# Fixed program order in beats, and transposes by DMA, in a fused attention and MoE kernel

## The chip, the cores and the metric

The kernel runs on one core of a Trainium2 chip. The metric is the device time of one execution in microseconds (us).

Names: PE is TensorE (matmul), DVE is VectorE, ACT is ScalarE, POOL is GpSimd, SP is the engine that here only issues DMAs. PSUM is the memory into which PE writes its products; here it is eight banks, each a buffer.

## The reference, cut to what matters

```python
def phi(x):
    proj = np.einsum('bhsd,df->bhsf', x, w_phi)
    proj = proj - np.max(np.abs(proj), axis=-1, keepdims=True)
    return np.concatenate([np.exp(proj), np.exp(-proj)], axis=-1)
q_p, k_p = phi(q), phi(k)
kv = np.einsum('bhsf,bhsd->bhfd', k_p, v);  z = np.sum(k_p, axis=2)
x = einsum(q_p, kv) / (einsum(q_p, z) + 1e-06)     # then (batch*seq, heads*dim) = 4608 x 512
h = x @ w_in                                       # 4608 x 2048, the "first product"
g = np.where(h > 0.0, h, np.exp(np.minimum(h, 0.0)) - 1.0)
out = g @ w_out                                    # 4608 x 512, the "second product"
```

There are 8 batches of 8 heads, 576 positions, head size 64 and 128 features. The kernel works on "quads", 4 heads of one batch, so there are 16 quads. A "slot" projects quad n and finishes quad n-1. A "chunk" is 512 rows of the MoE part, one for each batch and a ninth for the left-over rows.

## The kernel before

The projection of four head parts goes into a PSUM bank `pk`. Two engines read the bank: DVE takes the maximum `m_k`, ACT takes two exps. The exps do not use the maximum; it goes into a separate factor for v (`em`).

```python
def project(xT, hh, m):
    pk = apsum.tile([P, 4, F], FP32, name="pk", tag="ap")      # one of 4 attention banks
    ... nc.tensor.matmul(pk[...], xT[:, 2 * hh + j, :], w_phi_rhs, ...)
    nc.vector.tensor_reduce(m[...], pk[...], op=ALU.max, apply_absolute_value=True)
    return pk[...]

def k_head(hh):
    pk = project(st["kT"], hh, st["m_k"])
    for sg in range(2):
        nc.scalar.activation(dst, pk, ACT.Exp, scale=1.0 - 2.0 * sg)     # dst is EK
```

A piece of the first product crosses four engines. The bank `ph` is free again only after `gT` has been written:

```python
def mm1(ch, jt):
    ph = mpsum.tile([P, CHUNK], FP32, name="ph", tag="mp")     # one of 4 MoE banks
    ... 4 x nc.tensor.matmul(ph, w_in_sb[...], xTs[ch][:, ct, :], ...)
    nc.scalar.activation(e_sb, ph, ACT.Exp)
    nc.gpsimd.tensor_scalar(u_sb, e_sb, -1.0, 1.0, op0=ALU.add, op1=ALU.mult)
    nc.vector.scalar_tensor_tensor(gTs[ch][:, jt, :], u_sb, 0.0, ph, op0=ALU.min, op1=ALU.max)
```

k, q and x are transposed on PE, nine 128x128 blocks at a time, and copied out of PSUM by DVE (`tr`, `kT`, `qT`, `xT`). The program emits the steps of a slot with MoE units among them, and a list scheduler decides the order of the instructions on each engine.

Of the kernel before, what the change touches and what calls it, by code (L numbers as in the profile page):

```python
# [22 lines left out]
def kernel(  # L23
# [38 lines left out]
        tc.tile_pool(name="apsum", bufs=4, space=bass.MemoryType.PSUM)  # L62
    )
    mpsum = ctx.enter_context(
        tc.tile_pool(name="mpsum", bufs=4, space=bass.MemoryType.PSUM)
# [21 lines left out]
    xT_tail = consts.tile([P, N_CT, B * TAIL], BF16)  # L87
    xTs = {B: xT_tail}
# [31 lines left out]

    states = {}

    def attention_steps(i):
# [3 lines left out]
        def transposes(n):  # L127
# [4 lines left out]
            tr = apsum.tile([P, 8, P], BF16, name="tr", tag="ap")  # L132
            for j in range(8):
                o = m0 + j * P
                nc.tensor.transpose(tr[:, j, :], src[:, o:o + P], ident)  # L135
            copy = nc.scalar.copy if n == 1 and b == 0 else nc.vector.tensor_copy
            copy(dst[:, 0:8, :], tr)  # L137
            trt = apsum.tile([P, P], BF16, name="trt", tag="ap")
            nc.tensor.transpose(trt, src[:, t0:t0 + P], ident)
            copy(dst[:, 8, :], trt)  # L140
# [9 lines left out]
        def project(xT, hh, m):  # L150


            n = 2 if hh < 4 else 1
            pk = apsum.tile([P, 4, F], FP32, name="pk", tag="ap")
            for j in range(n):
                nc.tensor.matmul(  # L156
                    pk[:, 2 * j:2 * j + 2, :].rearrange("p a b -> p (a b)"),
                    xT[:, 2 * hh + j, :],
                    w_phi_rhs,
                    start=True,  # L160
                    stop=True,
                )
            o = (hh // 2) * NS + (hh % 2) * NT
            nc.vector.tensor_reduce(  # L164
                m[:, o:o + NT] if hh < 4 else m[:, NS - 1::NS],
                pk[:, 0:2 * n, :],
                axis=AX.X,
                op=ALU.max,
                apply_absolute_value=True,
            )  # L170
            return pk[:, 0:2 * n, :].rearrange("p a b -> p (a b)")

        def k_head(hh):
            pk = project(st["kT"], hh, st["m_k"])
            for sg in range(2):
                dst = st["EK"][:, hh, sg, :] if hh < 4 else st["EKt"][:, sg, :]
                nc.scalar.activation(dst, pk, ACT.Exp, scale=1.0 - 2.0 * sg)  # L177
# [31 lines left out]
        def q_features(par, c):  # L209
# [8 lines left out]
            for sg in range(2):  # L218
                nc.scalar.activation(  # L219
                    st["Eq"][:, par, c, sg, :], pq, ACT.Exp, scale=1.0 - 2.0 * sg  # L220
                )

        def q_features_tail():
# [9 lines left out]
            for sg in range(2):  # L233
                nc.scalar.activation(
                    st["Eqt"][:, sg, :],
                    pq.rearrange("p a b -> p (a b)"),
                    ACT.Exp,
                    scale=1.0 - 2.0 * sg,
                )
            w = small.tile([P, 2 * NS], FP32, name="w")  # L240
            nc.scalar.activation(w, st["m_q"], ACT.Exp, scale=2.0)
            st["w"] = w

        def kv(s):
# [27 lines left out]
            nc.scalar.copy(st["kv"][:, s], pkv)  # L272

        def out_head(hh):
# [5 lines left out]
            for sg in range(2):  # L280
# [14 lines left out]
            nc.vector.tensor_tensor(  # L295
                tot,
                pn[1],
                st["w"][:, o:o + NT, None].to_broadcast((P, NT, D1)),
                op=ALU.mult,
            )  # L300
            nc.vector.tensor_tensor(tot, tot, pn[0], op=ALU.add)  # L301

        def out_tail():
            pt = apsum.tile([P, 2, 2, D1], FP32, name="pnt", tag="ap")
            for s in range(2):
# [12 lines left out]
            nc.vector.tensor_tensor(  # L318
                tot,
                pt[:, 1],  # L320
                st["w"][:, NS - 1::NS, None].to_broadcast((P, 2, D1)),
                op=ALU.mult,
            )
            nc.vector.tensor_tensor(tot, tot, pt[:, 0], op=ALU.add)

        def divide():
# [4 lines left out]
            for c in range(2):  # L331
# [7 lines left out]

        def x_out():  # L340
            tr = apsum.tile([P, 8, P], BF16, name="tr", tag="ap")
            for j in range(8):
                nc.tensor.transpose(
                    tr[:, j, :],
                    st["x"][:, j].rearrange("p c d -> p (c d)"),
                    ident,
                )
            if qd == 0:
                xTs[b] = xtp.tile([P, N_CT, CHUNK], BF16, name="xT")
            nc.vector.tensor_copy(  # L350
                xTs[b][:, 2 * qd:2 * qd + 2, :],
                tr.rearrange("p (s t) n -> p s (t n)", s=2),
            )
            trt = apsum.tile([P, 2, TAIL], BF16, name="trt", tag="ap")
            nc.tensor.transpose(
                trt.rearrange("p s j -> p (s j)"),
                st["x"][:, 8].rearrange("p c d -> p (c d)"),
                ident,
            )
            nc.vector.tensor_copy(  # L360
                xT_tail[:, 2 * qd:2 * qd + 2, b * TAIL:(b + 1) * TAIL], trt
            )

        def each(f, *a):
# [12 lines left out]
            + [lambda: (out_tail(), divide())],  # L377
# [6 lines left out]
    def mm1(ch, jt):  # L384
# [3 lines left out]
        for ct in range(N_CT):  # L388
# [3 lines left out]
                xTs[ch][:, ct, :],  # L392
# [4 lines left out]
        nc.scalar.activation(e_sb, ph, ACT.Exp)  # L397
        u_sb = moesm.tile([P, CHUNK], BF16, name="u_sb")
        nc.gpsimd.tensor_scalar(  # L399
            u_sb, e_sb, -1.0, 1.0, op0=ALU.add, op1=ALU.mult  # L400
        )
        nc.vector.scalar_tensor_tensor(  # L402
            gTs[ch][:, jt, :], u_sb, 0.0, ph, op0=ALU.min, op1=ALU.max
        )

    def mm2(ch, tt):
        gT = gTs[ch]
        po = mpsum.tile([P, DM], FP32, name="po", tag="mp")
        for jt in range(N_JT):
            nc.tensor.matmul(  # L410
                po,
                gT[:, jt, tt * P:(tt + 1) * P],
# [3 lines left out]
            )  # L416
        o_sb = moesm.tile([P, DM], FP32, name="o_sb", bufs=2)
        nc.scalar.copy(o_sb, po)  # L418
        if ch < B:
            rows = out[ch * S:ch * S + MAIN, :].rearrange("(p t) o -> p t o", t=NT)  # L420
            nc.sync.dma_start(out=rows[:, tt, :], in_=o_sb)
        else:
# [6 lines left out]



    first, second = [], []
    run = [0]

    def moe_unit():
        if second and (not first or run[0] >= N_JT // 4):
            mm2(*second.pop(0))
            run[0] = 0
            return
        ch, jt = first.pop(0)  # L440
        mm1(ch, jt)
        run[0] += 1
        if jt == N_JT - 1:
            second.extend((ch, tt) for tt in range(CHUNK // P))
# [5 lines left out]
    quads = {}  # L450

    def chunk_ready(ch):
        first.extend((ch, jt) for jt in range(N_JT))

    def slot_steps(n):
        old, new, nxt = quads.get(n - 1), quads.get(n), quads.get(n + 1)
        if n == 0:
            return (
                new["k"] + new["scale"] + new["q"][:2] + nxt["tr"] + new["q"][2:]
                + new["vs"] + new["qf"]  # L460
            )
        if n == 1:
            steps = new["k"] + new["scale"] + old["kv"]
            for j in range(5):
                steps += new["q"][j:j + 1] + old["out"][j:j + 1]
                steps += new["vs"][j:j + 1]
            return steps + new["vs"][5:] + new["qf"] + nxt["tr"]
        if n == 2:

            return (  # L470
# [124 lines left out]
```

## Time and profile before

| | before |
|---|---|
| median of 4 runs | 447.31 us (445.98 to 448.27) |
| span of the profiled run | 445.4 us |
| PE busy | 396.4 us, 89% |
| slot, steady part (slots 5 to 14) | 22.54 us |

The table of waits sums, for every pair of a waiting and a releasing instruction, how long the engine stood: us in total, number of times, the longest. Three of its lines matter later:

```profile
DVE gT L402 <- POOL u_sb L399: 56.2, 55, 3.6
...
ACT EK L177 <- DVE m_k L164: 11.2, 8, 8.8
...
PE ph L389 <- DVE gT L402: 6.9, 11, 2.2
```

DVE often stands at gT for u_sb, but PE stands only 6.9 us in all for a gT: most of these waits hold nobody up. ACT's exps of k wait 11.2 us for DVE's maximum, 8.8 of it in one wait. The chain that ended last, by engine:

```profile
PE 54%; ACT 14%; DVE 13%; POOL 11%; issue 5%; DMA 1%; POOLq 0%; ACTq 0%
```

More than half of it is PE: the kernel is mostly bound by matmul work.

### The profile page before, as it was taken

The numbers are of one execution on the slowest core, as the hardware profiler recorded it, in microseconds if no ns is written. First come the engines' busy times: TensorE is split into PE (matmuls) and PEld (weight loads), VectorE is DVE, ScalarE is ACT, GpSimd is POOL, SyncE is SP. The second block draws the span as 40 slices with busy tenths as digits, with TensorE's granted clock in tenths as the row PEclk, the third lists the DMA queues.
The fourth block names the chain that finished last, engine by engine and source line by source line (L and its number), as shares of the span: only waits on it lengthen the run. The fifth ranks groups of instructions, "written<-read, shape, count | busy, mean of one in ns | idle before, by whom it ended". The sixth has DMA issues, their size and how long they took to land.

```text
span 445.4 us, 8463 instructions
## 1 busy us (share of the span) xinstructions
PE 396.4 (89%) x3194; PEld 221.5 (50%) x3248; DVE 283.8 (64%) x602; ACT 264.6 (59%) x585; POOL 243.8 (55%) x355
## 2 busy tenths in 40 slices
PE   3668659999999998999899989999889998999995
PEld 2445336555555455646465646554545454444442
DVE  2675859954897279927994589656978564443420
ACT  2854288745966487737775578566767733344331
POOL 9676078744694279446945494618283725342320
PEclk9955999999999999999999999999999999999999
DMA  8999929312830191119121912100000010011013
GB/s 135 215 186 233 227 28 106 107 49 58 98 107 25 71 108 55 55 71 132 23 86 56 145 28 83 48 25 25 2 0 25 25 42 32 24 50 47 25 47 71
DMA packets 45081, 33.12 MB, mean 74 GB/s; under 512 B 13904, under 2 KB 39632, under 8 KB 45040
## 3 DMA queue, kind: packets, MB, share of 16 engines
q0 software_dynamic: 28544, 14.82, 24.8%
q1 hardware_dynamic: 16496, 17.76, 12.9%
q8 instruction: 25, 0.41, 0.4%
q14 instruction: 16, 0.13, 0.1%
HBM read 36.77 MB, written 9.44 MB: 104 GB/s over the span
## 4 chain that ended last, share of the span: by engine, by line
PE 54%; ACT 14%; DVE 13%; POOL 11%; issue 5%; DMA 1%; POOLq 0%; ACTq 0%
PE po L410 24%; PE ph L389 13%; ACT EK L177 5%; ACT Eq L219 5%; POOL u_sb L399 4%; POOL vs L202 4%; PE pk L156 4%; DVE gT L402 4%; PE pkv L252 3%; PE tr L135 3%; ACT e_sb L397 2%; POOL x L333 2%; DVE m_q L164 2%; DVE m_k L164 2%; PE pn L285 2%
## 5 line engine op out<-in xcount | busy, mean ns | idle before, releaser
L399 POOL TENSOR_SCALAR u_sb<-e_sb 128x512 bf16<-128x512 f32 x144 | 87.7, 616 | 114.8 <-ACT e_sb L397 104.6
L389 PE MATMUL ph<-xT,w_in_sb 128*128 128x512 bf16 x480 | 130.5, 379 | 8.8 <-DVE gT L402 6.9
L410 PE MATMUL po<-w_out_sb,gT 128*128 128x512 bf16 x556 | 134.5, 379 | 0.8
L402 DVE SCALAR_TENSOR_TENSOR gT<-u_sb,ph 128x512 bf16<-128x512 bf16 x144 | 96.8, 681 | 56.8 <-POOL u_sb L399 56.2
L397 ACT ACTIVATE e_sb<-ph 128x512 f32<-128x512 f32 x144 | 86.4, 636 | 35.5 <-PE ph L389 33.0
L202 POOL TENSOR_TENSOR vs<-v_b,em 128x512 bf16<-128x512 f32 (+1 forms) x90 | 73.0, 830 | 27.4 <-ACT em L188 27.3
L410 PEld LDWEIGHTS <-gT 128*128 128x128 bf16 x576 | 54.5, 98 | 56.6 <-issue 1.0
L389 PEld LDWEIGHTS <-w_in_sb 128*128 128x128 bf16 x576 | 52.2, 97 | 52.3 <-issue 14.2
L219 ACT ACTIVATE Eq<-pq 128x512 bf16<-128x512 f32 x128 | 65.9, 639 | 15.5 <-PE pq L211 15.4
L177 ACT ACTIVATE EK<-pk 128x512 bf16<-128x512 f32 x128 | 68.0, 630 | 11.5 <-DVE m_k L164 11.2
L418 ACT COPY o_sb<-po 128x512 f32<-128x512 f32 x36 | 21.3, 593 | 83.9 <-PE po L410 66.7
L164 DVE TENSOR_REDUCE m_k<-pk 128x4 f32<-128x512 f32 (+1 forms) x80 | 49.0, 632 | 19.1 <-PE pk L156 18.7
L164 DVE TENSOR_REDUCE m_q<-pk 128x4 f32<-128x512 f32 (+1 forms) x80 | 49.4, 626 | 16.2 <-PE pk L156 16.0
L285 PEld LDWEIGHTS <-Eq 128*128 128x128 bf16 x512 | 30.2, 99 | 26.3 <-issue 10.5
L333 POOL TENSOR_TENSOR x<-tot,rec 128x576 bf16<-128x576 f32 x30 | 33.8, 1145 | 10.0 <-DVE rec L330 9.8
L285 PE MATMUL pn<-kv,Eq 128*128 128x65 bf16 x512 | 34.6, 196 | 4.9 <-DVE tot L295 1.1
L156 PE MATMUL pk<-w_phi_both,qT 128*128 128x256 bf16 x144 | 29.1, 288 | 4.4 <-ACT EK L177 2.2
L156 PE MATMUL pk<-w_phi_both,kT 128*128 128x256 bf16 x144 | 28.5, 287 | 3.2 <-ACT Eq L219 1.9
L295 DVE TENSOR_TENSOR tot<-pn,w 128x260 f32<-128x260 f32 x64 | 27.1, 424 | 5.6 <-PE pn L285 5.2
L137 DVE COPY kT<-tr 128x1024 bf16<-128x1024 bf16 x16 | 11.0, 688 | 29.8 <-PE tr L135 29.8
L301 DVE TENSOR_TENSOR tot<-tot,pn 128x260 f32<-128x260 f32 x64 | 26.7, 418 | 0.3
L252 PE MATMUL pkv<-vs,EK 128*128 128x65 bf16 x512 | 22.9, 198 | 1.9 <-ACT EK L177 1.2
(62 smaller groups left out, 358.8 us busy)
## 6 DMA issues: line engine op xcount, KB each, us to landing
out_dram<-o_sb SPq DMA_DIRECT2D x32, 256.0 KB, 2.3
v_b<-in_v_dram SPq DMA_DIRECT2D x7, 1024.0 KB, 5.7
k_b<-in_k_dram POOLq DMA_DIRECT2D x7, 512.0 KB, 6.9
q_b<-in_q_dram POOLq DMA_DIRECT2D x7, 512.0 KB, 7.7
w_in_sb<-in_moe_w_in_dram POOLq DMA_DIRECT2D x8, 256.0 KB, 7.8
w_out_sb<-in_moe_w_out_dram POOLq DMA_DIRECT2D x8, 256.0 KB, 11.9
v_b<-in_v_dram POOLq DMA_DIRECT2D x2, 512.0 KB, 6.4
out_dram<-o_sb SPq DMA_DIRECT2D x8, 128.0 KB, 2.4
```

The costliest lines, as they stand in the source:

```text
L156: nc.tensor.matmul(pk[:, 2 * j:2 * j + 2, :].rearrange("p a b -> p (a b)"), xT[:, 2 * hh + j, :], w_phi_rhs, start=True, stop=True,)
L164: nc.vector.tensor_reduce(m[:, o:o + NT] if hh < 4 else m[:, NS - 1::NS], pk[:, 0:2 * n, :], axis=AX.X, op=ALU.max, apply_absolute_value=True,
L177: nc.scalar.activation(dst, pk, ACT.Exp, scale=1.0 - 2.0 * sg)
L202: eng.tensor_tensor(st["vs"][:, sg, r, 0:D], kqv[b][2][:, o:o + n * D].rearrange("p (n d) -> p n d", d=D), st["em"][:, sg, r, None].to_bro ...
L219: nc.scalar.activation(st["Eq"][:, par, c, sg, :], pq, ACT.Exp, scale=1.0 - 2.0 * sg)
L285: nc.tensor.matmul(pt[:, t, :], st["Eq"][:, par, c, sg, o:o + P], st["kv"][:, s, c, sg, :], start=True, stop=True,)
L333: eng.tensor_tensor(st["x"][:, :, c, :], st["tot"][:, r, 0:D], rec[:, r, None].to_broadcast((P, NS, D)), op=ALU.mult,)
L389: nc.tensor.matmul(ph, w_in_sb[:, ct, jt * P:(jt + 1) * P], xTs[ch][:, ct, :], start=(ct == 0), stop=(ct == N_CT - 1),)
L397: nc.scalar.activation(e_sb, ph, ACT.Exp)
L399: nc.gpsimd.tensor_scalar(u_sb, e_sb, -1.0, 1.0, op0=ALU.add, op1=ALU.mult)
L402: nc.vector.scalar_tensor_tensor(gTs[ch][:, jt, :], u_sb, 0.0, ph, op0=ALU.min, op1=ALU.max)
L410: nc.tensor.matmul(po, gT[:, jt, tt * P:(tt + 1) * P], w_out_sb[:, jt, :], start=(jt == 0), stop=(jt == N_JT - 1),)
```

## The change

The intent: give every engine a fixed program order in the steady part, so that each consumer stands a fixed number of "beats" (16 in a slot) behind its producer; cut the MoE work into pieces of four matmuls that fill the beats evenly; and take the transposes of quads 3 to 15 (k, q) and batches 1 to 7 (x) off PE and DVE by DMA transposes issued from SP. The attention banks go from 4 to 5 and the MoE banks from 4 to 3. The core of the diff:

```diff
+    def post(lag, fn):                       # run fn `lag` beats later, in the order posted
+        if in_beats[0]:
+            agenda.setdefault(beat[0] + lag, []).append(fn)
+        else:
+            fn()
+    def next_beat():
+        beat[0] += 1
+        for fn in agenda.pop(beat[0], []):
+            fn()
...
+                nc.sync.dma_start_transpose(out=dst[:, 0:8, :], in_=src[:, m0:m0 + 8 * P])
+                nc.sync.dma_start_transpose(out=dst[:, 8, :], in_=src[:, t0:t0 + P])
...
-            nc.vector.tensor_reduce(...)
+            post(1, lambda: nc.vector.tensor_reduce(...))
+        def exps(psum, dst):
+            for sg in range(2):
+                post(1 + sg, lambda sg=sg: nc.scalar.activation(dst(sg), psum, ACT.Exp, ...))
...
-        nc.scalar.activation(e_sb, ph, ACT.Exp)
-        nc.gpsimd.tensor_scalar(u_sb, e_sb, ...)
-        nc.vector.scalar_tensor_tensor(gTs[ch][:, jt, :], u_sb, 0.0, ph, ...)
+        post(1, lambda: nc.scalar.activation(e_sb, ph, ACT.Exp))
+        post(1, lambda: nc.gpsimd.tensor_scalar(u_sb, e_sb, ...))
+        post(2, lambda: nc.vector.scalar_tensor_tensor(gTs[ch][:, jt, :], u_sb, 0.0, ph, ...))
...
+    tc.manual_schedule(engines={E.PE, E.DVE, E.Activation, E.Pool, E.SP})   # order as written
...
+        for t in range(BEATS):
+            next_beat()
+            for f in at[t]:
+                f()
+            now = n + (t + 1) / BEATS
+            due = (now - 2) * 32 / 3.25 if now < 5.25 else 32 + (now - 5.25) * 16.34
+            while done < due and (first or second):
+                moe_piece()
+                done += 1
```

## The prediction

> **What bounds the kernel now.** I read the page first, then the busy time of each engine by stage, then the PE timeline inside two stages, and only then the chain of waits.
>
> The page's busy shares:
>
> ```profile
> PE 396.4 (89%) x3194; PEld 221.5 (50%) x3248; DVE 283.8 (64%) x602; ACT 264.6 (59%) x585; POOL 243.8 (55%) x355
> ```
>
> PE leads, but its 89% is not a measure of full use: matmuls overlap. The five stages (columns: stretch, its length, busy us and instructions of PE, PEld, DVE, ACT, POOL, then PE clock, DMA share, GB/s):
>
> ```profile
> 0.00:51.00 51.00, 31.19 (x284) 20.82 (x286) 28.82 (x68) 23.83 (x55) 34.87 (x55) 0.80 1.14 200
> 51.00:109.50 58.50, 50.68 (x432) 29.01 (x437) 41.05 (x86) 40.06 (x93) 34.35 (x49) 1.00 0.47 80
> 109.50:335.00 225.50, 211.89 (x1866) 121.58 (x1899) 165.76 (x362) 152.83 (x347) 135.75 (x193) 1.00 0.31 62
> 335.00:375.00 40.00, 37.07 (x320) 20.40 (x326) 26.16 (x57) 21.73 (x46) 19.06 (x27) 1.00 0.08 28
> 375.00:446.00 71.00, 65.56 (x300) 29.66 (x303) 22.00 (x32) 26.13 (x44) 19.75 (x32) 0.99 0.15 45
> ```
>
> I chose the cuts at events: at 51 us the first projections of quad 2 begin (a quad is half a batch's heads, 16 quads in all; "slot n" is the stretch in which quad n is projected and quad n-1 finished); 109.5 and 335 are the kv products that open slots 5 and 15; from 375 only the two MoE products run. Half of the time is the third row, so that decides. The PE timeline shows its period and the true price of PE work:
>
> ```profile
> 109.55 0.67 PE L252 MATMUL pkv<-vs,EK 128*128 128x65 bf16 x16
> ...
> 248.00 0.61 PE L343 MATMUL tr<-ident,x 128*128 128x128 bf16 x8
> 248.45 0.22 PE L355 MATMUL trt<-ident,x 128*128 128x128 bf16 x1
> 248.50 0.67 PE L252 MATMUL pkv<-vs,EK 128*128 128x65 bf16 x16
> 249.11 0.29 PE L264 MATMUL pkv<-vs,EKt 64*128 64x65 bf16 x4
> ...
> 334.97 0.67 PE L252 MATMUL pkv<-vs,EK 128*128 128x65 bf16 x16
> ...
> 395.82 3.62 PE L389 MATMUL ph<-xT,w_in_sb 128*128 128x512 bf16 x16
> 399.28 3.62 PE L410 MATMUL po<-w_out_sb,gT 128*128 128x512 bf16 x16
> ```
>
> The reader should use starts, not durations. Nine transposes run from 248.00 to 248.50: 0.055 us each, where the group view says 0.22. Sixteen 512-wide matmuls take 399.28 - 395.82 = 3.46 us, 0.216 each. Slots 5 to 15 take (334.97 - 109.55)/10 = 22.54 us each. In the same way from dense stretches of this timeline: projection (256 wide) 0.11, feature matmul 0.216, kv for one half 0.61 + 0.23, four output matmuls 0.13.
>
> One slot of attention is then 18 x 0.11 + (4 x 0.216 + 0.11) + 2 x 0.84 + (8 x 0.13 + 0.26) = 5.9 us, plus 27 transposes x 0.055 = 1.5: 7.4 us. The MoE part of a slot is 136/14.5 = 9.4 units, of which one in five is 16 matmuls and the others 4: 60 matmuls, 13.0 us. So PE has 20.4 us of work in 22.54: about 2.1 us per slot are lost to waits, and PE is the bound but not tightly. The last row is PE alone at full rate, 0.216 per matmul.
>
> **What the Trainium skill says.** "Trainium Kernel Development and Optimization" (the note on reading a trace, at its head) warns that matmul busy time misleads because matmuls are pipelined; this trace agrees (0.055 against 0.22 us). "VectorE: DVE Perf Modes", section "The three transpose paths", gives for a 128x128 bf16 transpose 390 ns on TensorE and 1309 ns by the DMA crossbar: TensorE's figure must be a latency, as the trace shows 0.055 in a row; the DMA figure nothing in this trace tests. "DMA: Bandwidth & Descriptors", section "Latency and other measured facts", gives 261 GB/s for one strided DMA transpose: 256 KB would take an estimated 1.0 us of transfer by that figure. If instead 1309 ns were a price per block in a row, a slot's 27 blocks would need an estimated 35 us. The two disagree by ten times; this is the widest open point. No DMA transpose is in the trace of before.
>
> **The change, part by part.**
>
> *Removed:* 13 quads x 18 and 14 quads x 9 transposes leave PE: 360 x 0.055 = 20 us of PE. With them go the DVE copies, for these quads about 0.6 + 0.14 us three times a slot, some 30 us of DVE altogether, none of it on the bound except as a link: PE transpose, DVE copy, PE. PE work in all was 1152 x 0.216 + 16 x 7.4 = 367 us; it becomes 347.
>
> *Added:* 80 DMA transposes on SP's queue, three of 256 KB and three of 32 KB a slot. Those of k and q are issued at beats 3 and 6 of a slot of 16 beats and needed at the next slot's beat 0 or 2, at least 10 beats (12 us): hidden. Those of x are issued at beat 15; the chunk that reads them starts at beat 4, at most 5 beats, 6 us. Plain DMAs of before on the same queue:
>
> ```profile
> out_dram<-o_sb SPq DMA_DIRECT2D x32, 256.0 KB, 2.3
> v_b<-in_v_dram SPq DMA_DIRECT2D x7, 1024.0 KB, 5.7
> ```
>
> From these I estimate 3 to 5 us for x, mostly hidden.
>
> *Moved:* the list scheduler no longer orders engines after the opening. MoE goes into pieces of 4 matmuls (0.864 us); 32 of them up to slot 5.25, 16.34 a slot after that. By the end of slot 16 224 of 288 are done; the tail has 64. Before had 180 units of which 136 were done by then, about the same tail.
>
> The order of instructions shows something that the intent does not: first-product and second-product pieces hardly mix. From beat 4 of an odd slot come 16 first-product pieces, then 16 second-product ones, and, since 16.34 a slot is more than the 32 per batch available, beats 0 to 3 of later odd slots have no piece, with a burst of 3 to 5 following. So I price a pair of slots:
> - Second-product slot: PE 16.34 x 0.864 + 5.9 = 20.0 us; the others have far less. Bound: PE.
> - First-product slot: PE 20.0; DVE (0.60 apart in a row) 16 x 0.60 + 9 reductions 5.5 + combining and dividing 3.6 = 18.7; ACT (0.49 apart) 32 x 0.49 + 2.2 = 17.9; POOL 16 x 0.59 + 4.9 + 2.3 = 16.6. All near full, in order, with only three PSUM buffers for this product instead of four. One round trip is 0.86 + 0.17 on PE, 0.64 ACT, 0.62 POOL, 0.68 DVE, about 3.1 us with hand-overs; three buffers give 1.03 us a piece, within the beat of 1.22 but not within a burst.
>
> I allow 1.2 us a slot for these stalls and the starved beats: 21.2, against 22.54 now, while carrying 65 MoE matmuls instead of 60.
>
> *The sum:* opening as before, 51 (its instructions are the same, plus a fifth attention bank); slots 2 to 5.25 with PE 9.85 x 0.864 + 5.9 = 14.4 and ACT nearly as much, latency added, 16.5 x 3.25 = 54; 10.75 slots x 21.2 = 228; slot 16, without new projections, 17.5; wait for the last x before chunk 7, 3; tail 64 x 0.864 = 55.3 plus 16 pieces bound by three buffers, 16 x 0.17 = 2.7: 58; last copy and store 4.5 (before: last matmul ends at 440.9 of 445.4). Total 416; I say 415.
>
> **Rivals.**
> 1. *The beats work as designed.* Speaks for it: every engine is under PE's 20.0 us a slot. Then 20.2 a slot and no wait for x: 217 + 17 + 56 + 51 + 52 + 4.5 = 398.
> 2. *In-order stalls eat it.* A list-scheduled PE could run something else at each wait; the fixed order can't. For it: three buffers, all engines at 83 to 94% in first-product slots, starved beats; the profile of before already has 56 us of DVE idle behind u_sb and 33 of ACT behind ph. At 22.5 a slot, as now: 242 instead of 228, and slower early slots: 432.
> 3. *DMA transposes become the bound.* If blocks cost 1309 ns in a row, 35 us a slot, over 550. At 5 us per large one, a slot has 15 us plus the 6 us loads, close to the limit, and x arrives late: six chunks x 3 us more, 433. Against: the DMA share of 0.31 in the steady stage leaves room.
> 4. *Only the transposes' time is saved,* 20 us of PE, order worth nothing: 427.
>
> **Range and chances.** Rivals 1 and 2 bound the likely outcomes: 396 to 436. The 2% line is 437.9; beyond it only rival 3 or a bad rival 2 goes. Faster 0.87, same 0.08, slower 0.05.
>
> **What would show it.** Right: the first-slot kv products of the steady stage about 21 us apart; no PE wait on kT or qT; even slots near 20, odd ones 22 or more; PE's waits in odd slots on DVE gT and ACT exps. The tail's first 16 pieces should be about 1.03 us apart. It is wrong if PE waits on SP's transposes, if the large ones take over 6 us to land, or if slots 2 to 4 take 20 us each.

## The result, and the profile after

| | before | after |
|---|---|---|
| median of 4 runs | 447.31 us (445.98 to 448.27) | 483.11 us (480.93 to 483.18) |
| span of the profiled run | 445.4 us | 481.3 us |
| opening, up to the first beat | 51 us | 57 us |
| slots 2 to 4 | 58.5 us | 62.4 us |
| slot, steady part | 22.54 us (slots 5 to 14) | 25.4 us (slots 5 to 15) |

The changed kernel is slower by 7.9%: ratio 1.0791, 95% interval 1.0748 to 1.0833. Ratios here are the mean time of one kernel's fast runs over that of the other's of the same rounds, so not quite the ratio of the medians quoted.

PE's busy time, then the stages (columns as in the prediction: stretch, length, busy us and instructions of PE, PEld, DVE, ACT, POOL, PE clock, DMA share, GB/s). The cuts are the first beat, the kv products that open slots 5 and 16, and the end:

```profile
PE 389.0 (81%) x2888; PEld 206.3 (43%) x2888; DVE 265.8 (55%) x522; ACT 270.1 (56%) x585; POOL 244.6 (51%) x355
```

```profile
0.00:57.00 57.00, 32.21 (x286) 22.17 (x287) 29.68 (x71) 24.09 (x56) 30.53 (x49) 0.73 1.08 170
57.00:119.35 62.35, 48.50 (x348) 25.21 (x347) 36.75 (x69) 39.57 (x89) 35.35 (x51) 0.89 0.56 77
119.35:398.89 279.54, 234.56 (x1857) 125.22 (x1856) 171.09 (x336) 178.66 (x393) 155.53 (x220) 0.99 0.53 95
398.89:481.30 82.41, 73.69 (x401) 33.66 (x399) 28.31 (x47) 27.73 (x49) 23.23 (x37) 1.00 0.19 46
```

No engine is full in the second and third rows: PE is busy for 78% and 84% of them. A stage in which nobody is full is one in which engines wait for each other in turn. The last row is as predicted. PE's granted clock was 0.89 in slots 2 to 4, against 1.00 there before, and 0.99 in the third row, so a lower clock is not what makes the steady slots long. The kv products of three slots show where it happens within a pair of slots:

```profile
350.35 0.67 PE L286 MATMUL pkv<-vs,EK 128*128 128x65 bf16 x16
...
370.99 0.67 PE L286 MATMUL pkv<-vs,EK 128*128 128x65 bf16 x16
...
398.89 0.67 PE L286 MATMUL pkv<-vs,EK 128*128 128x65 bf16 x16
```

Slot 14, which holds second-product pieces, took 20.64 us; slot 15, with first-product pieces, took 27.90. The waits that grew:

```profile
DVE gT L450 <- POOL u_sb L444: 115.1, 101, 7.5
ACT EK L207 <- DVE m_k L192: 61.7, 42, 10.4
...
PE ph L432 <- DVE gT L450: 32.3, 47, 2.0
```

DVE's wait at gT doubled (56.2 to 115.1), ACT's wait for the maximum went from 8 times to 42 (11.2 to 61.7 us), and PE now pays 32.3 instead of 6.9. The chain that ended last is no longer mostly PE:

```profile
PE 37%; POOL 21%; DVE 15%; issue 15%; DMA 7%; ACT 4%; SPq 1%; POOLq 0%; ACTq 0%; DVEq 0%
```

One turn of what happens, from the timeline of slot 2 (start, duration, engine, line, operation; in brackets how long the engine stood and who released it):

```profile
65.57 0.69 DVE L450 SCALAR_TENSOR_TENSOR gT<-u_sb,ph 128x512 bf16<-128x512 bf16 x1 [1.86 <-POOL u_sb L444]
66.17 0.69 DVE L192 TENSOR_REDUCE m_k<-pk 128x4 f32<-128x512 f32 x1
...
66.89 0.60 ACT L207 ACTIVATE EK<-pk 128x512 bf16<-128x512 f32 x1 [1.57 <-DVE m_k L192]
...
67.39 0.59 ACT L441 ACTIVATE e_sb<-ph 128x512 f32<-128x512 f32 x1
...
68.07 0.61 POOL L444 TENSOR_SCALAR u_sb<-e_sb 128x512 bf16<-128x512 f32 x1 [1.31 <-ACT e_sb L441]
...
68.71 0.69 DVE L450 SCALAR_TENSOR_TENSOR gT<-u_sb,ph 128x512 bf16<-128x512 bf16 x1 [1.85 <-POOL u_sb L444]
```

Read it downward. DVE finishes gT and only then takes the maximum m_k. ACT's exp waits for that maximum. ACT's e_sb of the next piece stands behind the exp. POOL's u_sb waits for e_sb, and DVE's next gT for u_sb, with the next maximum behind it. That is a loop: from gT to gT 68.71 - 65.57 = 3.14 us, for one piece and one k part, where the prediction had counted 1.22 us a piece. Two of its links are data (e_sb to u_sb to gT). Two are order within an engine (gT before m_k on DVE, EK before e_sb on ACT). The fifth, EK behind m_k, is neither: the exp does not use the maximum. The Trainium skill explains that one: "PSUM — Partial Sum Buffer", section "PSUM bank collisions raise a hardware error", says that the compiler adds a dependency between any two instructions on different engines that touch the same bank and quadrant, reads included. Both read the bank `pk`, and the trace agrees in the 1.57 us above and in the 61.7 us of the table. No run took this link away.

In the median the DMA transposes themselves look well. From the list of DMAs (issuing queue, count, size, median us from the start of the issue to landing; no size is printed for transposes):

```profile
out_dram<-o_sb SPq DMA_DIRECT2D x32, 256.0 KB, 2.7
...
kT<-k_b SPq DMA_TRANSPOSE x26, 3.1
qT<-q_b SPq DMA_TRANSPOSE x26, 3.1
xT<-x SPq DMA_TRANSPOSE x14, 3.4
xT_tail<-x SPq DMA_TRANSPOSE x14, 2.4
```

### The profile page after: what moved, and what is told of

Same layout as the page of the kernel before. It is cut to its first block, busy times and chain, and to the rows that moved or that the text cites. A ratio compares the mean times of both kernels' runs of the same rounds, so it can differ in the third digit from the quotient of the medians.

```text
span 481.3 us, 7888 instructions
## 1 busy us (share of the span) xinstructions
PE 389.0 (81%) x2888; PEld 206.3 (43%) x2888; DVE 265.8 (55%) x522; ACT 270.1 (56%) x585; POOL 244.6 (51%) x355
## 3 DMA queue, kind: packets, MB, share of 16 engines
q0 software_dynamic: 28544, 14.82, 23.6%
## 4 chain that ended last, share of the span: by engine, by line
PE 37%; POOL 21%; DVE 15%; issue 15%; DMA 7%; ACT 4%; SPq 1%; POOLq 0%; ACTq 0%; DVEq 0%
PE po L463 21%; POOL u_sb L444 12%; PE ph L432 7%; DVE gT L450 6%; DMA q_b<-in_q_dram 3%; POOL vs L242 3%; PE pk L182 3%; POOL x L377 3%; DMA xT<-x 2%; ACT EK L207 2%; DVE tot L337 2%; DVE tot L331 2%; DVE m_q L192 2%; DVE m_k L192 2%; PE pq L251 2%
## 5 line engine op out<-in xcount | busy, mean ns | idle before, releaser
L432 PE MATMUL ph<-xT,w_in_sb 128*128 128x512 bf16 x512 | 134.8, 393 | 38.9 <-DVE gT L450 32.2
L450 DVE SCALAR_TENSOR_TENSOR gT<-u_sb,ph 128x512 bf16<-128x512 bf16 x144 | 97.0, 683 | 115.9 <-POOL u_sb L444 115.1
L463 PE MATMUL po<-w_out_sb,gT 128*128 128x512 bf16 x576 | 140.9, 379 | 0.0
L207 ACT ACTIVATE EK<-pk 128x512 bf16<-128x512 f32 x128 | 70.8, 612 | 61.9 <-DVE m_k L192 61.7
L432 PEld LDWEIGHTS <-w_in_sb 128*128 128x128 bf16 x576 | 57.3, 99 | 108.2 <-issue 60.7
L207 ACT ACTIVATE Eq<-pq 128x512 bf16<-128x512 f32 x128 | 73.0, 610 | 21.1 <-PE pq L251 20.9
L182 PE MATMUL pk<-w_phi_both,qT 128*128 128x256 bf16 x144 | 30.4, 288 | 7.3 <-ACT EK L207 3.7
L319 PEld LDWEIGHTS <-Eq 128*128 128x128 bf16 x512 | 27.0, 103 | 20.0 <-issue 8.7
L319 PE MATMUL pn<-kv,Eq 128*128 128x65 bf16 x512 | 30.1, 201 | 5.0 <-DVE m_q L192 1.7
L331 DVE TENSOR_TENSOR tot<-pn,w 128x260 f32<-128x260 f32 x64 | 27.0, 423 | 10.2 <-PE pn L319 10.1
L251 PE MATMUL pq<-qT,w_phi_both 128*128 128x512 bf16 x64 | 25.1, 404 | 5.9 <-DVE tot L331 2.1
L182 PEld LDWEIGHTS <-qT 128*128 128x128 bf16 x144 | 14.4, 102 | 25.4 <-issue 13.5
```

Source lines behind the costliest of these rows:

```text
L182: nc.tensor.matmul(pk[:, 2 * j:2 * j + 2, :].rearrange("p a b -> p (a b)"), xT[:, 2 * hh + j, :], w_phi_rhs, start=True, stop=True,)
L207: lambda sg=sg: nc.scalar.activation(dst(sg), psum, ACT.Exp, scale=1.0 - 2.0 * sg),
L319: nc.tensor.matmul(pt[:, t, :], st["Eq"][:, par, c, sg, o:o + P], st["kv"][:, s, c, sg, :], start=True, stop=True,)
L331: nc.vector.tensor_tensor(tot, pn[1], st["w"][:, o:o + NT, None].to_broadcast((P, NT, D1)), op=ALU.mult,)
L432: nc.tensor.matmul(ph, w_in_sb[:, ct, jt * P:(jt + 1) * P], xTs[ch][:, ct, :] if ch < B else xT_tail[:, ct // 2, :, ct % 2, :], start=(ct ...
L450: lambda: nc.vector.scalar_tensor_tensor(gTs[ch][:, jt, :], u_sb, 0.0, ph, op0=ALU.min, op1=ALU.max),
```

## The experiments

The theory after this reading: the fixed order has a loop, gT, m_k, EK, e_sb, u_sb, gT, and breaking any of its links that is only order should bring time back. The rivals: the DMA transposes cost time; three MoE banks are too few; the lumps (16 first-product pieces, then 16 second-product ones) are the cost; any fixed order loses against the list scheduler. Each kernel gave correct results and was run for three rounds. The runs of one group shared a chip and the runs of the kernel before.

### First group: which half of the change

**dma_only**: the kernel before, list-scheduled, with the DMA transposes alone.

```diff
 # kernel before
+            if i >= 3:
+                nc.sync.dma_start_transpose(out=dst[:, 0:8, :], in_=src[:, m0:m0 + 8 * P])
+                nc.sync.dma_start_transpose(out=dst[:, 8, :], in_=src[:, t0:t0 + P])
...
+            if b > 0:
+                nc.sync.dma_start_transpose(out=main, in_=x[:, 0:8 * P])
+                nc.sync.dma_start_transpose(out=tail, in_=x[:, 8 * P:])
+                return
```

> The kernel before, list-scheduled, with the change's DMA transposes of k, q and x and nothing else of it. Theory (the fixed order costs the time, the transposes are innocent): 20 us of PE work go and little comes back, 425 to 440 us, ratio to before 0.95 to 0.985. Rival (the transposes cost it: late xT and kT, DMA contention with the loads): 455 us or more.

Measured: 479.83 us (478.88 to 481.6), ratio 1.0718. This half alone, under the list scheduler, costs as much as the whole change. By itself that would speak for the rival that DMA transposes cost time; the next run forbids so simple a reading.

**beats_pe**: the changed kernel with all transposes back on PE.

```diff
-            if i < 3:
+            if True:
...
-            if b > 0:
+            if False:
```

> The changed kernel with all its transposes back on PE, the beats kept. Theory (fixed order): the beats alone already lose; PE has the transposes to do again but is idle a fifth of the time, so 485 to 505 us. Rival (DMA transposes are the cost): at or below the kernel before, under 455 us.

Measured: 517.44 us (516.7 to 520.0), ratio 1.1567, above the 485 to 505 expected. Within the fixed order the DMA transposes save 517 - 483 = 34 us. The two halves do not add: each alone is slower than the kernel before, and the second makes the first better. What costs is the rest of the change, fixed order, pieces and banks together: 69 us over the kernel before with the same transposes.

**free_order**: the changed kernel without the fixed order, so that the scheduler may move instructions again.

```diff
-    ctx.enter_context(
-        tc.manual_schedule(engines={E.PE, E.DVE, E.Activation, E.Pool, E.SP})
-    )
```

> The changed kernel with the fixed program order of the steady part lifted: same instructions emitted in the same sequence, same pools, but the list scheduler may reorder each engine. Theory (in-order head-of-line waits between DVE, ACT and POOL): most of the loss comes back, 420 to 445 us; the 3.1 us period of the first MoE slot goes. Rival (the loss lies in the lumpy placing of MoE pieces, or in three PSUM buffers, whatever the order): 465 us or more.

Measured: 474.66 us (472.63 to 475.28), ratio 1.059. Freedom brings back only 2 points of the 7.9: the expected 420 to 445 us failed, and the time lies in the rival's range of 465 or more. The trace says why this time is no test of the loop. DVE's wait for u_sb fell to 93.4 us and ACT's for the maximum to 30.7, and the period of 3.14 us is gone from slot 2 (gT starts at 70.94, 72.14 and 73.07). But the first of these gT had waited 10.12 us for a u_sb that stood on POOL behind loads of k and q, and PE's own wait for gT rose to 39.7. So the loop shrank and something else came, which dma_only, list-scheduled with the same transposes and as slow, has too (below).

**mpsum4**: 4 attention and 4 MoE banks, as before.

```diff
-        tc.tile_pool(name="apsum", bufs=5, space=bass.MemoryType.PSUM)
+        tc.tile_pool(name="apsum", bufs=4, space=bass.MemoryType.PSUM)
-        tc.tile_pool(name="mpsum", bufs=3, space=bass.MemoryType.PSUM)
+        tc.tile_pool(name="mpsum", bufs=4, space=bass.MemoryType.PSUM)
```

> The changed kernel with four PSUM buffers for the MoE products and four for attention, as before, in place of three and five. Theory (a chain of in-order waits from beat to beat): in the k beats nothing changes, since the chain e_sb, u_sb, gT, reduction, exp is what takes 3.1 us, not the buffer; in the q beats the POOL order holds at 1.6 us a beat; the fifth attention buffer is missed; 475 to 490 us. Rival (the round trip over three buffers is the bound): a quarter of the first-product slots' excess goes, 455 to 468 us.

Measured: 488.3 us (487.37 to 488.36), ratio 1.0898. The fourth bank takes PE's wait for gT away (32.3 to 2.7 us) and leaves the loop as it was: in slot 2 gT starts at 62.80 and 65.94, again 3.14 us apart. PE stands elsewhere instead: its projections' wait for EK went from 10.1 to 18.3 us, that for m_q from 1.1 to 11.9. So too few MoE banks do not make the loop. What a fourth one would bring by itself was not measured, for the attention has one bank less here.

### Second group: the link on ACT, and the lumps

**esb_first**: e_sb is emitted at the head of its beat, ahead of the exps on ACT. The exp and its wait stay, but e_sb no longer stands behind them.

```diff
+        for fn in ahead.pop(beat[0], []):      # in next_beat, before the agenda
+            fn()
...
-        post(1, lambda: nc.scalar.activation(e_sb, ph, ACT.Exp))
+        ahead.setdefault(beat[0] + 1, []).append(
+            lambda: nc.scalar.activation(e_sb, ph, ACT.Exp)
+        )
```

> The changed kernel with one order changed on ACT: in every beat the MoE exponential e_sb is put ahead of the attention exponentials instead of behind them. Theory (in the beats with k heads a loop closes through gT, reduction, EK exp, e_sb, u_sb, gT, 3.14 us a beat, because the exp must wait for the reduction of the same PSUM bank and e_sb stands behind it): cutting the loop brings slots 2 and 3 from 22 to 24 us down to 16 to 19, and a few us in later slots: 455 to 467 us. Rival (the loop is not it; POOL's order or lumpy pieces hold every beat): 474 us or more.

Measured: 462.96 us (461.23 to 464.69), ratio 1.0302. One link of the loop turned round brings back 4.9 points, some 20 us, and the period goes: in slot 2 gT starts at 58.06, 59.80, 61.77 and 63.63, some 1.9 us apart. ACT's wait for the maximum fell from 61.7 to 25.7 us, DVE's for u_sb from 115.1 to 88.9. Slot 3, where k parts and first-product pieces meet, went from 23.7 to 19.5 us.

**balanced**: first- and second-product pieces alternate, with the second product one chunk behind.

```diff
-            due = (now - 2) * 32 / 3.25 if now < 5.25 else 32 + (now - 5.25) * 16.34
-            while done < due and (first or second):
+            due = (now - 2) * 16 / 3.25 if now < 5.25 else 16 + (now - 5.25) * 16
+            while done < due and first:
```

> The changed kernel with first-product and second-product pieces alternating (the second product lags its chunk by a whole chunk; 16 pieces a slot, none starved or bunched; 16 pieces more in the tail, about 14 us). Theory (lumps: slots full of first-product pieces run at POOL's 1.6 us a beat and at a round trip of 4 to 4.5 us over three buffers, and PE has nothing else): slots from 5 on come to 20 to 21 us instead of 25.4, 440 to 455 us. Rival (every beat pays the chain whatever its piece): slots stay at 24 or more, 480 us or more with the longer tail.

Measured: 508.01 us (507.66 to 508.49), ratio 1.1305, in the rival's range. With the lumps gone the kernel is 25 us slower still. Now every slot has first-product pieces among its k parts, and every one pays the loop:

```profile
DVE gT L450 <- POOL u_sb L444: 197.9, 141, 3.6
...
ACT EK L207 <- DVE m_k L192: 90.4, 44, 10.4
```

141 of the 144 gT waited. The lumps had been hiding part of the loop, since in slots of second-product pieces nothing closes it. As the main cost they fall.

**esb_balanced**: both edits together.

```diff
 # esb_first, and
+            due = (now - 2) * 16 / 3.25 if now < 5.25 else 16 + (now - 5.25) * 16
+            while done < due and first:
```

> Both edits together. Theory: they cut different waits, the sum of both gains: 425 to 445 us, slots at PE's own 20 us. If the two gains are one and the same, within 1% of the better of the two alone.

Measured: 469.93 us (469.55 to 470.75), ratio 1.0459, far above the sum of gains that was expected. Turning e_sb round is worth 38 us here against 20 in the lumpy kernel: where the loop is met more often, breaking a link is worth more. The alternation itself still costs 7 us over esb_first.

**dma_bufs3** belongs to another question, why dma_only lost; it is told with the fourth and fifth groups.

### Third group: the link on DVE, with a control

The edit of DVE's order was made with 16 pieces a slot in place of 16.34, so that no beat is left without a piece, and so it needs a control.

**rate16**: the changed kernel with 16 pieces a slot.

```diff
-            due = ... 32 + (now - 5.25) * 16.34
+            due = ... 32 + (now - 5.25) * 16
```

> The changed kernel with 16 MoE pieces a slot from slot 5.25 on instead of 16.34, so that no beat is without a piece and none has a bunch; four pieces more in the tail (3.5 us). It is the control for the next three. Theory (the beat-to-beat chain costs, starved beats little): within 1.5% of the changed kernel, 476 to 490 us. Rival (bunches after starved beats cost about 3 us in each odd slot): 460 to 472 us.

Measured: 496.4 us (495.73 to 496.61), ratio 1.1074, above the range expected. The prediction had counted beats without a piece as a cost. The opposite holds: at 16.34 the pieces of the first product had crowded into beats after the k parts; at an even rate they reach into the k beats of the following slot and pay the loop there. Second-product slots went from 20.6 to 23.8 us up to 25.8 to 26.6, and ACT's wait for the maximum from 61.7 to 80.6. Part of the 13 us may be the clock: in slots 5 to 15 the granted one was 0.95 here and 0.99 in the changed kernel.

**gt_last**: as rate16, with gT emitted after the other work of its beat, so that DVE takes the maximum first. gT then stands behind all other DVE work of the beat: both reductions, m_k and m_q, and the combining of the outputs (`tot`).

```diff
 # rate16, and
+        for fn in last.pop(beat[0], []):       # in next_beat, after the agenda
+            fn()
...
-        post(
-            2,
+        last.setdefault(beat[0] + 2, []).append(
             lambda: nc.vector.scalar_tensor_tensor(
                 gTs[ch][:, jt, :], u_sb, 0.0, ph, op0=ALU.min, op1=ALU.max
-            ),
+            )
         )
```

> As the control, but gT is emitted behind the other DVE work of its beat instead of ahead of it. Theory (gT at the head of DVE waits 1.5 to 2.7 us for u_sb with the reductions and combinations of the next beat behind it, and these hold up the exps on ACT, the PSUM buffers and so PE): 430 to 450 us, DVE's wait for u_sb falls from 115 us to under 50, ACT's wait for m_k from 62 to under 20. Rival (POOL's order in first-product slots is the bound): slots 2 and 3 gain, the odd slots stay at 26 us or more: 460 us or more.

Measured: 449.9 us (447.88 to 450.99), ratio 1.0035. This order on DVE is worth 496.4 - 449.9 = 46.5 us of the same rounds, and the kernel is back at the time of before. Nothing was added, removed or given another buffer. The main proof of the loop is its period, at the same place in slot 10, rate16 first:

```profile
254.37 0.69 DVE L450 SCALAR_TENSOR_TENSOR gT<-u_sb,ph 128x512 bf16<-128x512 bf16 x1 [0.21 <-POOL u_sb L444]
...
257.51 0.69 DVE L450 SCALAR_TENSOR_TENSOR gT<-u_sb,ph 128x512 bf16<-128x512 bf16 x1 [1.85 <-POOL u_sb L444]
258.11 0.68 DVE L192 TENSOR_REDUCE m_k<-pk 128x4 f32<-128x512 f32 x1
260.65 0.69 DVE L450 SCALAR_TENSOR_TENSOR gT<-u_sb,ph 128x512 bf16<-128x512 bf16 x1 [1.85 <-POOL u_sb L444]
261.25 0.68 DVE L192 TENSOR_REDUCE m_q<-pk 128x4 f32<-128x512 f32 x1
262.24 0.69 DVE L450 SCALAR_TENSOR_TENSOR gT<-u_sb,ph 128x512 bf16<-128x512 bf16 x1 [0.30 <-POOL u_sb L444]
```

```profile
230.27 0.68 DVE L453 SCALAR_TENSOR_TENSOR gT<-u_sb,ph 128x512 bf16<-128x512 bf16 x1
...
232.21 0.69 DVE L453 SCALAR_TENSOR_TENSOR gT<-u_sb,ph 128x512 bf16<-128x512 bf16 x1
232.81 0.68 DVE L196 TENSOR_REDUCE m_q<-pk 128x4 f32<-128x512 f32 x1
234.10 0.69 DVE L453 SCALAR_TENSOR_TENSOR gT<-u_sb,ph 128x512 bf16<-128x512 bf16 x1 [0.60 <-POOL u_sb L448]
```

In rate16 the next gT comes 3.14 us later where DVE takes an m_k in between, and 1.59 us later where it takes an m_q, whose bank no exp reads. gT is ahead both times, so it is the way over the exp that makes the period. In gt_last the same steps are 1.94 and 1.89 us apart. Not all of the 46.5 us need be the loop: gT also went behind m_q and `tot`, and in slots 5 to 15 the granted clock was 0.95 in rate16 and 0.99 in gt_last (PE busy 242.1 and 229.2 us for the same matmuls). Against the changed kernel, at 0.99 too, gt_last gains 483.11 - 449.9 = 33 us. The waits, rate16 first:

```profile
DVE gT L450 <- POOL u_sb L444: 130.4, 108, 7.5
ACT EK L207 <- DVE m_k L192: 80.6, 49, 9.9
```

```profile
DVE gT L453 <- POOL u_sb L448: 71.9, 81, 7.5
ACT EK L211 <- DVE m_k L196: 47.6, 35, 10.4
```

Both fell by 58.5 and 33.0 us, though to more than the 50 and 20 expected: the direction held and the size missed. The slots are now 23.5 (first-product) and 21.1 us.

**gt_last_m4**: gt_last with 4 and 4 banks.

```diff
 # gt_last, and
-        tc.tile_pool(name="apsum", bufs=5, space=bass.MemoryType.PSUM)
+        tc.tile_pool(name="apsum", bufs=4, space=bass.MemoryType.PSUM)
-        tc.tile_pool(name="mpsum", bufs=3, space=bass.MemoryType.PSUM)
+        tc.tile_pool(name="mpsum", bufs=4, space=bass.MemoryType.PSUM)
```

> As gt_last with four PSUM buffers for the MoE products and four for attention. Theory: with gT later the product needs a buffer longer, so a fourth one now helps: 1 to 3% less than gt_last. Rival (attention's buffers are the shorter ones): more than gt_last by 1 to 3%.

Measured: 460.27 us (459.12 to 463.09), ratio 1.0281. With the loop broken the fourth MoE bank again shortens PE's wait for gT (18.5 to 3.5 us), but PE's wait of the k and q projections for EK goes from 2.9 to 14.1, and the kernel loses 10 us. In this order the attention's banks are the shorter ones, as the rival had it, and 5 and 3 is the better choice.

**gt_last_esb**: both links turned round.

```diff
 # gt_last, and
-        post(1, lambda: nc.scalar.activation(e_sb, ph, ACT.Exp))
+        ahead.setdefault(beat[0] + 1, []).append(
+            lambda: nc.scalar.activation(e_sb, ph, ACT.Exp)
+        )
```

> As gt_last with e_sb ahead on ACT as well. Theory: once gT stands last, the loop is already open, and e_sb ahead gives nothing more or makes exps wait for a matmul: within 1.5% of gt_last. Rival (two separate losses): another 10 us or more.

Measured: 442.96 us (441.58 to 443.93), ratio 0.9883. The two do not add (46 and 20 would be 66; together they give 53), as two cuts of the same loop should; the 20 was measured at 16.34 pieces a slot, so the sum is rough. The 6.9 us that e_sb adds lie at the edge of the 1.5% expected, below the rival's 10. Second-product slots are 20.2 us, PE's work in them; first-product slots still 23.6.

### Why first-product slots stay long

There is a second limit, and the timeline of the changed kernel already has it. In beats 8 to 12 of a slot POOL scales v, with pieces between:

```profile
341.91 1.04 POOL L242 TENSOR_TENSOR vs<-v_b,em 128x512 bf16<-128x512 f32 x1
342.92 0.62 POOL L444 TENSOR_SCALAR u_sb<-e_sb 128x512 bf16<-128x512 f32 x1
343.50 1.04 POOL L242 TENSOR_TENSOR vs<-v_b,em 128x512 bf16<-128x512 f32 x1
344.52 0.62 POOL L444 TENSOR_SCALAR u_sb<-e_sb 128x512 bf16<-128x512 f32 x1
```

POOL does not stand, and its u_sb come 344.52 - 342.92 = 1.60 us apart: for these beats POOL is the bound, one piece in 1.60 us. Over four such beats, and one of 1.31 us with the two small vs, that is an estimated 4 x (1.60 - 1.22) + 0.09 = 1.6 of the 3.5 us by which the first-product slots of gt_last_esb are longer; the rest was not separated. The chain that ended last in gt_last_esb agrees: in slot 11 it runs almost on POOL alone, over vs, u_sb and x, from 256.63 to 266.81 us. It is not to be seen in POOL's busy share (51%), nor in its sum over a slot. Spreading the first product over both slots should hide it, now that the loop is broken.

### Fourth group: alternation in the good order, and the transposes again

**all3**: both links turned round, and the pieces alternating.

```diff
 # gt_last_esb, and
+            due = (now - 2) * 16 / 3.25 if now < 5.25 else 16 + (now - 5.25) * 16
+            while done < due and first:
```

> gT last, e_sb ahead, and first- and second-product pieces alternating. Theory (the excess left in first-product slots is POOL's u_sb and vs at 1.6 us a beat; alternating halves u_sb's density): slots 5 to 15 all at 20 to 20.8 us in place of 23.6 and 20.1, minus 6 x 3 us, plus 12 pieces (10 us) more in the tail, shorter early slots: 430 to 441 us. Rival (something else holds odd slots): 445 us or more.

Measured: 432.4 us (430.7 to 432.66), ratio 0.9638 (0.9609 to 0.9666). The alternation that cost 25 us in the changed kernel (12 against the control rate16) now saves 10.6. Slots 6 to 15 take 20.88 us each (336.79 - 127.97 over ten), against 24.83 in the changed kernel. The page and the waits:

```profile
PE 378.5 (88%) x2888; PEld 206.7 (48%) x2888; DVE 265.0 (61%) x522; ACT 265.9 (62%) x585; POOL 243.8 (57%) x355
```

```profile
DVE gT L459 <- POOL u_sb L454: 101.1, 104, 3.0
...
ACT EK L215 <- DVE m_k L200: 9.7, 14, 1.3
...
PE ph L440 <- DVE gT L459: 3.3, 6, 0.6
```

DVE stands at gT for 101.1 us, nearly as long as in the slow kernel, and it does not matter, because nothing that anyone waits for stands behind it: PE's wait for gT is 3.3 us and ACT's for the maximum 9.7. The length of a wait is not its cost.

**good_pe**: gt_last_esb with all transposes on PE.

```diff
 # gt_last_esb, and
-            if i < 3:
+            if True:
...
-            if b > 0:
+            if False:
```

> gt_last_esb with all transposes on PE again. Theory (PE is the bound again once the beats flow, so 20 us of PE work and the DVE copies come back in full): 462 to 475 us. Rival (the transposes were only worth the waits they stood in, about 34 us in the changed kernel for that reason): under 455 us.

Measured: 474.68 us (472.99 to 478.57), ratio 1.0576. In the good order the DMA transposes are worth 474.7 - 443.0 = 32 us, as much as the 34 in the bad one, and more than the 20 us of PE work that they remove. The trace names some of the rest: DVE waits 35.2 us for the transposes of x on PE, and PE's weight loads for those wait 16.1 us for POOL's x. In a fixed order every PE transpose stands between matmuls and waits for x in place. It also shows that beats in good order, with transposes on PE, are still slower than the list scheduler.

**x_dma** and **kq_dma**: the list-scheduled kernel with only x, or only k and q, by DMA.

```diff
 # dma_only, for x_dma
-            if i < 3:
+            if True:
 # dma_only, for kq_dma
-            if b > 0:
+            if False:
```

> The kernel before, list-scheduled, with only x transposed by DMA from batch 1 on. Theory (the loss of dma_only comes from the k and q transposes, for whose reads the next batch's loads wait on POOL's queue): 440 to 450 us, within 1.5% of before. Rival (late x or SP's queue behind stores): 455 us or more.

> The kernel before, list-scheduled, with only k and q transposed by DMA from quad 3 on. Theory: the loss of dma_only is here, 465 to 482 us. Rival: 455 us or less.

Measured: x_dma 443.06 us (442.06 to 443.32), ratio 0.9879; kq_dma 473.79 us (472.69 to 475.51), ratio 1.0572. Under the list scheduler DMA transposes of x gain 5 us and those of k and q lose 25. So the loss of dma_only lies with k and q.

### Why k and q by DMA lose under the list scheduler: left open

The trace of dma_only shows POOL standing at the loads of the next k and q until SP's transposes have read the old ones out of the same buffer, with u_sb behind:

```profile
POOL q_b L103 <- DMA qT<-q_b: 22.4, 3, 7.8
...
POOL k_b L103 <- DMA kT<-k_b: 9.6, 1, 9.6
```

The theory from this: POOL's queue stands at a load, and the first product behind it. Two runs were to take that wait away.

**dma_bufs3** (run with the second group): a third buffer for k and q.

```diff
 # dma_only, and
-            stage.tile([P, BW + 4 * D], BF16, name="k_b"),
-            stage.tile([P, BW + 4 * D], BF16, name="q_b"),
+            stage.tile([P, BW + 4 * D], BF16, name="k_b", bufs=3),
+            stage.tile([P, BW + 4 * D], BF16, name="q_b", bufs=3),
```

> The kernel before with the DMA transposes alone, now with three buffers for k_b and q_b instead of two. Theory (POOL's in-order queue stands at a load of k_b or q_b until a transpose on SP's queue has read the buffer, with u_sb behind it; 22 + 14 + 10 us of such waits in the run with two): 440 to 455 us, that is most of its loss of 32 us goes. Rival (late kT, qT, xT, or transfers in each other's way): 470 us or more.

Measured: 475.03 us (473.13 to 477.6), ratio 1.0556, 1.6 points better than dma_only and far from the 440 to 455 expected. POOL's waits at loads for a transpose fell from 22.4 + 9.6 to 15.6 us. The scheduler put loads still earlier, and PE's longest wait for gT became 17.07 us.

**loads_late** (fifth group): dma_only with the loads given out one slot later.

```diff
 # dma_only, and
-            extra += load_kq(n // 2 + 1)
...
+        if n % 2 == 1 and 1 < (n + 1) // 2 < B:
+            extra += load_kq((n + 1) // 2)
```

> As dma_only (list-scheduled, all three DMA transposes), with the loads of k and q given out one slot later, so that the buffers have been read when POOL comes to them. Theory (the load standing on POOL's queue with u_sb behind it was the loss): the PE waits of 13.7, 7.3 and 7.5 us for gT go, 430 to 450 us. Rival (late qT and kT by themselves): 460 us or more.

Measured: 481.15 us (479.67 to 482.64), ratio 1.0748, where 430 to 450 us were expected. The scheduler left the loads on POOL nearly where they had been, and the waits stayed. One of them:

```profile
66.69 0.91 POOL L103 DMA_DIRECT2D q_b<-in_q_dram  x1 [4.07 <-issue]
...
71.00 1.21 POOL L401 TENSOR_SCALAR u_sb<-e_sb 128x512 bf16<-128x512 f32 x2
```

In the same stretch PE stood 12.49 us at ph, for gT. The picture fits the theory, but loads_late removed nothing of what it was to remove and dma_bufs3 only half, so neither tests it. In kq_dma, which loses the 25 us alone, only 6.2 us of POOL's waits at these loads are put down to a transpose, and 30.9 to m_k, pq and gT of other engines. That POOL's loads in the list-scheduled order cause the 25 us is suggested by traces and not shown. In the changed kernel the loads have fixed beats, and no such wait is among its largest.

### Fifth group: one more step

**usb_ahead**: all3 with u_sb ahead of the other POOL work of its beat.

```diff
 # all3, and
-        post(
-            1,
+        ahead.setdefault(beat[0] + 1, []).append(
             lambda: nc.gpsimd.tensor_scalar(
                 u_sb, e_sb, -1.0, 1.0, op0=ALU.add, op1=ALU.mult
-            ),
+            )
         )
```

> As all3, with u_sb ahead of the attention work of its beat on POOL as well. Theory (with the pieces alternating POOL has slack): within 1% of all3, 428 to 437 us. Rival (vs ahead of u_sb still delays gT): 424 us or less.

Measured: 430.07 us (429.23 to 433.48), ratio 0.9631 (0.958 to 0.9682), the same as all3 within the intervals. Both beat the kernel before, by some 3.7%.

One more way to cut the loop, the reductions in their own beat with no lag, was not run.

## Why the prediction was wrong, point by point

**The end and the whole.** Predicted 415, range 396 to 436; measured 483.11. Stage by stage, from the rows above: the opening 57 us against 51; slots 2 to 4 62.4 against 3 x 16.5 = 49.5; slots 5 to 15 279.5 against 0.25 x 16.5 + 10.75 x 21.2 = 232; slot 16, the wait for x and the tail 82.4 against 17.5 + 3 + 58 + 4.5 = 83. The misses are 6, 13 and 47.5 us; the rest was right.

**The step that failed** is the pricing of waits in first-product slots: "One round trip is 0.86 + 0.17 on PE, 0.64 ACT, 0.62 POOL, 0.68 DVE, about 3.1 us with hand-overs; three buffers give 1.03 us a piece, within the beat of 1.22", and from it "I allow 1.2 us a slot for these stalls". It counts a trip as if each engine were free when a piece arrives, and three pieces in flight as if they were independent. The runs showed two things in its place. First, a loop of order that lets one piece through in 3.14 us wherever a k part meets a first-product piece; its fifth link, the exp behind the reduction of the same bank, was not in the prediction at all, although the trace of before had 11.2 us of it. Putting m_k ahead of gT on DVE took the period from 3.14 to 1.9 us and, with the rest of gT's new place, brought back 46.5 us; e_sb ahead on ACT alone brought back 20. Second, POOL's 1.60 us a piece while v is scaled. The allowance that was needed is 25.4 - 20.0 = 5.4 us a slot, not 1.2. The same omission explains 16.5 for slots 2 to 4, where k parts and first-product pieces meet: "latency added" was a word where a loop should have been traced.

**Beats without a piece** were counted as a cost. The control at 16 pieces a slot, without them, was 13 us slower, part of it perhaps by the clock.

**Slips.** (334.97 - 109.55)/10 is the mean of slots 5 to 14, not 5 to 15, and 2% below 447.31 is 438.4, not 437.9; neither changes anything.

**Removed and added.** PE work of 347 us against 367 could not be checked by busy time, for matmuls overlap; DVE's busy time fell by 18.0 us where some 30 were counted; the trade of the transposes is worth 32 to 34 us in a fixed order, more than the 20 counted, for the in-order waits at PE's transposes go too. The landing was estimated at 3 to 5 us for x and measured at a median of 3.4 (2.4 to 3.1 for the others), with single ones of 7.2 for x, 12.5 for k and 15.5 for q; PE waited for a transposed k once, 0.8 us, and only a weight load for a q, 0.2; x cost it 6.7 us in two waits, against the 3 allowed.

**The rivals.** Rival 3, DMA transposes as the bound, was rightly held unlikely for the changed kernel. Under the list scheduler those of k and q did cost 25 us, which the prediction had no reason to ask. Rival 2 named the mechanism, in-order stalls, and even the waits to look at, but sized it at 22.5 us a slot and 432. Rival 1, the beats as designed, needs another order: all3 runs at 20.88 us a slot where it said 20.2. Rival 4 was wrong in its premise, that order is worth nothing: order alone, gT's place on DVE and e_sb's on ACT, was worth 53 us (clock included, as said above).

**The signs named.** Second-product slots near 20: slots 12 and 14 had 20.6, others up to 23.8. First-product slots at 22 or more: 26.4 to 28.4 from slot 7 on. PE's waits there on gT: yes. The tail's first 16 pieces about 1.03 us apart: three pieces every 3.19 us, 1.06. Of the signs of error, slots 2 to 4 at 20 us each came true in the mean, 62.35/3 = 20.8, and PE did wait on SP's transposes, 7.5 us in all. The prediction had thus named the place where it would fail, and not traced it.

**Left open.** The opening is 6 us longer and its granted clock lower (0.73 against 0.80); PE waits there for loads of k and q. No run separates these, nor what the lower clock in slots 2 to 4 (0.89 against 1.00) did to them.

## What to carry to other kernels

Before fixing an order, write down for each engine what stands behind each instruction that may wait, and follow the edges through all engines, order and data and shared PSUM banks alike: a closed path is a period, and a fourth MoE bank did not shorten this one (mpsum4). In each beat, let an engine first do what others wait for (here reductions and e_sb) and last do what ends a chain (here gT). And judge two edits together as well as apart: alternation cost 25 us with the loop and saved 10.6 without it, and the same transposes by DMA were a loss of 32 us under one order and a gain of 32 under another.

## What the Trainium skill lacked or had wrong

- "VectorE: DVE Perf Modes", section "The three transpose paths", gives 390 ns (TensorE) and 1309 ns (DMA) for a 128x128 block, and does not say that neither is a price per block in a row. TensorE's came 0.055 us apart in the trace of before; by DMA one block (xT_tail) landed in 2.4 us and eight (xT) in 3.4, so an estimated 0.14 us for each further block and a fixed part above 2 us, 1.23 of it the issue on SP.
- "DMA: Bandwidth & Descriptors", section "Latency and other measured facts", gives 261 GB/s for a strided DMA transpose. From the same two rows, 224 KB more in 1.0 us are an estimated 229 GB/s: near it, but at 256 KB the fixed part is most of the 3.4 us.
- "Advanced Engine Details and Errata", section "X-Bar Transpose (TRN2)", says that transpose DMAs are as fast as regular ones. In the changed kernel a 256 KB one landed in 3.4 us from the start of its issue and a plain 256 KB store in 2.7. But the issue took 1.26 and 0.34 us of these (medians), so after it an estimated 2.1 and 2.4 us are left: the transfer agrees, and what the section leaves out is the longer issue.
- "PSUM — Partial Sum Buffer", section "PSUM bank collisions raise a hardware error", has the dependency between two readers of one bank, but not what it does to a program in fixed order: the exp of ACT stood 61.7 us behind a maximum that it does not use, and closed a loop of 3.14 us.
- No page gives a price for a load that is issued from an engine that also computes and has to wait for its buffer: POOL stood 22.4 and 9.6 us at such loads of k and q in the list-scheduled kernel with DMA transposes.
